# Eleven fill matmuls at two places of the table build, and the first product's matmuls in front in each sum on TensorE

## The chip, the cores and the metric

The kernel runs on one core of one Trainium2 chip. The metric is the device time of one execution in microseconds (us); the median of several runs is compared. The engines are TensorE (PE in the profile, its weight loads PEld), VectorE (DVE), ScalarE (ACT), GpSimd (POOL) and SyncE (SP, which issues most DMAs).

## The reference

Four layers over x of 2048 rows and 512 columns, bf16, two kinds in turn:

```python
x = A_u
x = x + _A_ref(_layernorm(x), A_re, A_im, B_re, B_im, C_re, C_im, log_dt, Dskip)
x = x + _B_ref(_layernorm(x), wqkv, wo)
x = x + _A_ref(_layernorm(x), ...same parameters...)
x = x + _B_ref(_layernorm(x), wqkv, wo)
```

`_A_ref` is a state-space convolution along the rows. For every column d it forms a kernel K[d, l] = Re sum over n of C[d,n] * exp(dt*A[d,n]*l) * dt*B[d,n], with 128 complex modes n and 2048 lags l, multiplies by it with FFTs, and adds u * Dskip. `_B_ref` is attention with 32 heads, in which each row looks at 8 earlier rows, two apart. The convolution kernel K depends on the parameters alone, so it is built once and serves both A layers.

## The kernel before

**The stage that matters here** is the first one, `kgen`, which builds the spectrum of K. The powers exp(dt*A*l) are not formed for 2048 lags. A lag is split as u + 8v, and two tables of complex powers are filled, U (20 lags u) and V (32 lags v), for 128 modes on the partitions. This is done in four quarters c of 128 columns d. The tables have two buffers, U[c % 2] and V[c % 2], so quarter 2 can fill its tables only when quarter 0's were read. A product of U and V on TensorE over the modes then gives K at all lags. It goes through DRAM into another layout (`rows`), and a second matmul with a constant matrix G gives the spectrum, which is stored to DRAM (`kt_scratch`) and loaded later by the convolution (`Kt`).

**Order by hand.** `KGEN` is a string of words, and each word issues a few instructions; every engine carries out its own in the order of the words. A number after the colon is the quarter.

- `U512p:1`, `v8p:0` and the like: one doubling step of a table. VectorE multiplies a part of the table that is filled by a power, `prod[0]` by its real part and `prod[1]` by its imaginary part (both real and imaginary rows r of the source; lines 489, 495, 497), in a scratch ring of 8192 elements that lies in tile Z.
- `%name`: the two products are added or subtracted on VectorE (L507).
- For a step with a p at its end: `+name` adds them on TensorE instead (`sum_pe`, L521 and L522): a matmul of each product with the identity or the negative identity into one PSUM tile `psadd`. `=name` copies the sum into the table on ScalarE (L528, L531). A step of over 512 columns has `+0name`, `+1name` for the two rows r, each of two pieces of at most 512 columns; the others do both rows in one word.
- `v16yn:c`, `v16xn:c`: the last doubling of V, four VectorE multiplications each (L476), into V and a second table `Vsecond`.
- `pcq`: the product of V and U for quarter c and sixteen of its 64 column pairs, q from 0 to 3 (`product`, L561 and, for the skip term, L565). p03 and p02 need `v16yn:0`, p00 and p01 need `v16xn:0`.
- `kcm` copies the product (L572) and, after the second of a quarter, issues the DMAs through DRAM (L580, L583). `scI` is the spectrum matmul (L594, L599), `ocI` and `ecI` its copies and stores (L610, L618, L623, L604).
- `nJ` and `nJa` are the statistics of the first layer norm (L190, L191 on ScalarE, L185 to L187 on VectorE), `qI`, `mI`, `lI`, `bI` the ladder of squared powers, `c0` to `c2` the last lag, `Aa:c`, `Ba:c`, `ua:c` copies that begin a table.
- `w03:n`: a fill. TensorE multiplies the identity by itself, n columns in matmuls of up to 512, into the PSUM tile that p03 will overwrite (`warm`, L548). Nothing reads the result.

A product's place in the scratch ring is written again some steps later. The ring starts anew where a step doesn't fit, so `v8p:1` writes where `v8p:0` had its products: its `prod[0]` has to wait until the sums `+0v8p:0` and `+1v8p:0` have read the old `prod[0]`, and its `prod[1]` the same for the old one.

The tile of a sum comes from a pool of two PSUM buffers (`psg`), shared with the spectrum matmuls; a third sum waits until ScalarE has copied the first out.

After `kgen` come the convolution (transposes, loads of Kt, multiplication on VectorE, inverse), the attention layer, and both again. They are not touched.

Of the kernel before, what the change touches and what calls it, by code (L numbers as in the profile page):

```python
# [305 lines left out]
def a_layer(nc, tc, C, Xg, Ng, kt_dram, layer, Z, es_z, a=None):  # L306
# [24 lines left out]
    def y_rows(g, hf):  # L331
# [17 lines left out]
           "256": (256, (P0 - 2, 1, 4), (0, 6)), "1024": (1024, (P0, 2, 2), (8,)), "512": (512, (P0, 1, 6), (10,))}  # L349
U_AFTER = {"4": (), "2": ("4",), "1": ("2",), "256": ("2",), "1024": ("256",), "512": ("1024", "256")}  # L350
QC = DCH // 2
KGEN = ("m0 q0 b0 x1 l0 m1 q1 x0 t l1 b1 x3 x2 q2 m2 b2 l2 x5 m3 U4p:1 q3 U4:0 l3 b3 %U4:0 u:1 m4 q4 u:0 l4 b4 m5 q5 U2p:0 l5 "
# [18 lines left out]
PLUS = (13,)  # L371
WHOLE = (1, 2, 3, 4, 5, 6)
FIRST_LOADS = [("rows_end", 3), ("rows_end", 3), ("stored", 2, 2), ("stored", 3, 2)]
# [3 lines left out]
def kgen(nc, tc, C, prm, kt_dram, Zf, norm_row, norm_rstd, norm_apply, norm_apply_row, norm_tiles, load_rest, es_a, es_y, open_conv):  # L377
    everything = KGEN.split()
    with ExitStack() as es:
# [64 lines left out]
        def psum():  # L444
            if not late.get("psum"):
                es_t.close()
                late["psum"] = pool("k_psk", 2, space=PSUM), pool("k_psg", 2, es_y, space=PSUM, side="right")
            return late["psum"]
# [65 lines left out]
        def sum_pe(name, c, rs):  # L514
            prod, out, hn, f, size = sums[name, c]
            ps = tiles["+", name, c, rs] = psum()[1].tile([128, 2, 512], F32, name="psadd", tag="psg")
            for r in rs:
                for k, c0 in enumerate(range(0, size, 512)):
                    s = slice(c0, min(c0 + 512, size))
                    b = r if len(rs) == 2 else k  # L520
                    nc.tensor.matmul(ps[:, b, 0:s.stop - c0], C["ident"][:], prod[0][:, r, s], start=True, stop=False)  # L521
                    nc.tensor.matmul(ps[:, b, 0:s.stop - c0], C["ident" if r else "nident"][:], prod[1][:, 1 - r, s], start=False, stop=True)  # L522

        def sum_out(name, c, rs):
            prod, out, hn, f, size = sums[name, c]
# [154 lines left out]
        for c in range(4):  # L680
# [16 lines left out]
            for full in [n for n in everything if n.endswith(f":{c}") and n[0] in "Uv"]:  # L697
                name = full.split(":")[0]
                key = name.rstrip("xypn")
                if key[0] == "U":  # L700
                    needs = (["x5", *free] if key == "U4" else [f"{base['u']}:{c}"]) + [log2[int(key[1:])]] + in_quarter(c, *["U" + k for k in U_AFTER[key[1:]]])
                else:
                    m = int(key[1:])
                    needs = (["b3", "b4", *free] if m == 2 else [f"{base['A']}:{c}", log2[8 * m]]) + ([f"{base['B']}:{c}"] if m > 4 else []) + in_quarter(c, *[f"v{k}" for k in (2, 4, 8) if k < m])
                    if name[-1] == "n":
                        needs += ["y"] + (["prep"] if c % 2 else [])
                word(full, lambda name=name, c=c: step(name, c, sums), *needs)
                if name[-1] not in "pn":
                    word("%" + full, lambda name=name, c=c: sum_dve(name, c), full)
                for rs in ([(0, 1)] if small(name) else [(0,), (1,)]) if name[-1] == "p" else []:  # L710
                    tag = "" if len(rs) == 2 else str(rs[0])
                    word("+" + tag + full, lambda name=name, c=c, rs=rs: sum_pe(name, c, rs), full, "x5")
                    word("=" + tag + full, lambda name=name, c=c, rs=rs: sum_out(name, c, rs), "+" + tag + full)
# [899 lines left out]
```

## Time and profile before

| | |
|---|---|
| median of 3 runs | 438.28 us (436.13 to 438.46) |
| the profiled execution | 439.68 us, its span 437.9 us |
| TensorE, busy share of the span | 87% |
| VectorE | 92% |
| ScalarE | 75% |
| TensorE clock granted, mean | 0.977 |

The span runs from the first instruction to the last, and the time around it is 1.78 us in the profiled execution. A row of the timeline has the start, the duration, engine, line and operation, what is written and read, the count, and in brackets how long the engine had stood idle and what ended that. A matmul's duration includes its way through the array, so it overlaps the next one: the distance of two starts is what it occupies. A row of the windows has the stretch, its length, busy time and number of instructions of each engine, the mean clock granted to TensorE in that stretch (PEclk, 1.00 or 0.50 where nothing changes in it), and the DMA share.

### The profile page before, as it was taken

What the parts mean: (1) busy time and instruction counts of PE and PEld (TensorE: products, weight loads), DVE (VectorE), ACT (ScalarE), POOL (GpSimd) and SP (SyncE); (2) the same over time, 40 slices, a digit from 0 to 9 for tenths busy, and PEclk for the clock granted to TensorE, in tenths of its full rate; (3) what the DMA queues carried; (4) which work ended last, traced back from release to release, by engine and by line L of the source; (5) the groups of instructions that cost most, each with busy time, mean ns of one, the idle gap of its engine ahead of it and who ended that gap; (6) DMA issues with size and microseconds to landing.
All of it is one profiled execution on the core that took longest, in us unless ns stands there. A gap on an engine that the chain in (4) does not pass through costs nothing.

```text
span 437.9 us, 12189 instructions
## 1 busy us (share of the span) xinstructions
PE 379.9 (87%) x5045; PEld 259.3 (59%) x5084; DVE 402.4 (92%) x783; ACT 329.6 (75%) x604; POOL 25.5 (6%) x66
## 2 busy tenths in 40 slices
PE   1176799999989989999997899789899999996995
PEld 1032586676468745686685465367746578784562
DVE  6999989999889969799999999999789999999993
ACT  6999979998989979755665399979969666652442
POOL 5000002001210000020010000000000002020000
PEclk9998779999999999999999899999999999999998
DMA  7900001254889930016043007458100003562022
GB/s 237 419 10 0 1 3 44 74 168 115 250 241 274 297 117 4 1 31 140 3 89 82 0 4 217 168 153 277 57 0 3 1 1 62 110 115 56 1 98 98
DMA packets 25647, 44.06 MB, mean 101 GB/s; under 512 B 7285, under 2 KB 17206, under 8 KB 24950
## 3 DMA queue, kind: packets, MB, share of 16 engines
q1 hardware_dynamic: 22630, 37.30, 29.4%
q0 software_dynamic: 1856, 4.53, 4.4%
q10 hardware_dynamic: 1104, 1.44, 0.9%
q8 instruction: 40, 0.66, 0.7%
q14 instruction: 17, 0.14, 0.1%
HBM read 29.01 MB, written 6.95 MB: 82 GB/s over the span
## 4 chain that ended last, share of the span: by engine, by line
PE 44%; DVE 21%; ACT 21%; issue 7%; DMA 6%; SPq 0%; POOL 0%; DVEq 0%; ACTq 0%; POOLq 0%
PE ps_qk L1170 10%; DVE prodpv L1352 7%; PE ps_v L1257 5%; PE psk L561 4%; DVE prodqk L1220 3%; PE Lp L1242 3%; PE psg L594 3%; ACT xc L272 3%; ACT Z L1426 3%; DVE Z L497 2%; PE pt L254 2%; PE vp L290 2%; PE xp L266 2%; DMA V<-V 2%; ACT X L1406 2%
## 5 line engine op out<-in xcount | busy, mean ns | idle before, releaser
L1352 DVE TENSOR_TENSOR prodpv<-V,Lsb 128x512 bf16<-128x512 bf16 (+1 forms) x124 | 79.4, 701 | 1.2 <-PE po L1362 1.1
L1170 PE MATMUL ps_qk<-xnT,wqk 128*128 128x512 bf16 x256 | 60.3, 379 | 0.0
L1362 PE MATMUL po<-halves,prodpv 128*128 128x64 bf16 x1024 | 38.9, 193 | 7.4 <-DVE prodpv L1352 5.8
L1218 DVE TENSOR_TENSOR prodqk<-qT,N 128x1024 bf16<-128x1024 bf16 (+3 forms) x88 | 42.5, 539 | 2.6 <-ACT N L1173 2.2
L1362 PEld LDWEIGHTS <-prodpv 128*128 128x128 bf16 x1024 | 34.8, 98 | 16.5 <-DVE prodpv L1352 11.1
L279 DVE TENSOR_TENSOR pab<-xc,Kt 128x2048 bf16<-128x2048 bf16 (+1 forms) x34 | 39.2, 1160 | 2.9 <-ACT xc L272 2.8
L1220 DVE TENSOR_TENSOR prodqk<-qT,N 128x512 bf16<-128x512 bf16 (+3 forms) x56 | 40.6, 762 | 0.7 <-ACT N L1173 0.6
L1373 ACT CAST oT<-po 128x512 bf16<-128x512 f32 x32 | 18.3, 595 | 27.4 <-PE po L1362 27.4
L1170 PEld LDWEIGHTS <-wqk 128*128 128x128 bf16 x256 | 23.9, 97 | 23.8
L272 ACT CAST xc<-xp 128x1024 bf16<-128x1024 f32 (+1 forms) x34 | 34.3, 1020 | 4.1 <-PE pt L254 2.8
L299 ACT CAST VT<-vp 128x1024 bf16<-128x1024 f32 (+1 forms) x32 | 33.2, 1052 | 3.1 <-PE vp L290 3.1
L290 PE MATMUL vp<-sb_IC,pab 128*128 128x128 bf16 x512 | 33.8, 219 | 1.2 <-ACT VT L299 0.4
L290 PEld LDWEIGHTS <-pab 128*128 128x128 bf16 x512 | 30.6, 98 | 6.0 <-issue 1.9
L1242 PEld LDWEIGHTS <-prodqk 128*128 128x128 bf16 x1024 | 29.6, 96 | 4.1 <-DVE prodqk L1218 0.6
L1242 PE MATMUL Lp<-sb_bones,prodqk 128*128 128x8 bf16 x1024 | 30.5, 166 | 0.2 <-DVE prodqk L1220 0.2
L1257 PE MATMUL ps_v<-wv,xnT 128*128 128x256 bf16 x256 | 30.4, 272 | 0.0
L521 PE MATMUL psadd<-Z,sb_ident 128*128 128x512 bf16 (+3 forms) x49 | 17.8, 376 | 12.6 <-DVE Z L497 8.2
L1389 PE MATMUL ps_o<-wo_t,oT 128*128 128x512 bf16 x91 | 26.4, 396 | 0.8 <-issue 0.2
L1257 PEld LDWEIGHTS <-xnT 128*128 128x128 bf16 x256 | 24.3, 97 | 3.6
L1173 ACT CAST qT<-ps_qk 128x512 bf16<-128x512 f32 x32 | 18.8, 593 | 7.5 <-PE ps_qk L1170 7.5
L1123 DVE BATCH_NORM_STATS2 ln_stats<-X 128x6 f32<-128x512 bf16 x37 | 23.7, 675 | 0.8 <-ACT X L1447 0.8
L1281 POOL DMA_DIRECT2D V<-V x16 | 8.9, 561 | 255.8 <-ACT V L1264 228.4
(201 smaller groups left out, 854.1 us busy)
## 6 DMA issues: line engine op xcount, KB each, us to landing
Kt<-kt_scratch SPq DMA_DIRECT2D x60, 256.0 KB
kt_scratch<-ks SPq DMA_DIRECT2D x32, 128.0 KB
G<-c_G SPq DMA_DIRECT2D x2, 1536.0 KB
V<-V SPq DMA_DIRECT2D x8, 288.0 KB
X<-in_A_u_dram SPq DMA_DIRECT2D x4, 512.0 KB
F1Tsb<-c_F1T SPq DMA_DIRECT2D x2, 1024.0 KB
V<-V SPq DMA_DIRECT2D x4, 512.0 KB
V<-V POOLq DMA_DIRECT2D x4, 384.0 KB, 7.3
```

The source lines that it names most:

```text
L272: nc.scalar.copy(xc[:, gs].rearrange("q g o l -> q (g o l)"), xp[:].rearrange("q h n -> q (h n)")[:, gs.start * 128:gs.stop * 128])
L279: nc.vector.tensor_tensor(pab[:, gs], xc[:, gs].to_broadcast([128, n, 2, 128]), kt[:, gs], ALU.mult)
L290: nc.tensor.matmul(vp[:, g, :], pab[:, g, ab, :], C["IC"][:, ab, :], start=(ab == 0), stop=(ab == 1))
L299: nc.scalar.copy(dst[..., gs], src[..., gs])
L1170: nc.tensor.matmul(t.ps[:], wqk[:, ct, f0:f0 + 128], x_group(g)[:, :, ct], start=(ct == 0), stop=(ct == 3))
L1218: nc.vector.tensor_tensor(b.pr[:, u:u + 2 * n, 1 - halves_of[0], :], q, cols(kT[i][:, starts[0]:starts[0] + n * 128]), ALU.mult)
L1220: nc.vector.tensor_tensor(b.pr[:, u:u + 2 * n].rearrange("f u a q -> f a u q")[:, ::-1], q.unsqueeze(1).to_broadcast([128, 2, 2 * n, 64]), ...
L1242: nc.tensor.matmul(t.Lp[:, w, u % 2, u // 2, :], b.pr[:, u].rearrange("f a q -> f (a q)"), bones[:], start=False, stop=(t.parts == W // 2 ...
L1257: nc.tensor.matmul(t.ps[:, jj, :], tokens(ct, jp * 2 + jj, c), wv[:, ct, fp * 256:(fp + 1) * 256], start=(jj + ct == 0), stop=(jj == 1 and ...
L1352: nc.vector.tensor_tensor(t.p2[:, c:c + k, 0:nj, :].rearrange("p c j (d h) -> p c j d h", d=DH), m.V2[i // 2][:, c0 + c:c0 + c + k, r0:r0 ...
L1362: nc.tensor.matmul(po[jj // k][:, jj % k, c, :], t.p2[:, c - c0, jj, :], fold, start=(first and c == c0 and jj % k == 0), stop=(last and c ...
L1389: nc.tensor.matmul(t["ps"][:], m.oT[:, ft, j * 128:(j + 1) * 128], wo_t[:, ft, :], start=(added and ft == 0), stop=False)
```

## The change

Two edits.

1. In `KGEN`, `w03:1536` (three matmuls of 512 columns) is put behind `=U256p:0`, ahead of `+0v8p:0`, and `w03:4096` (eight matmuls of 512 columns) behind `U512p:1`, ahead of `p03`. The words around them:

```diff
-... Ba:0 +U256p:0 w03:384 l9 =U1p:1 b10 v8p:0 =U256p:0 +0v8p:0 U1024p:1 Ba:1 +1v8p:0 U1024p:0 ...
+... Ba:0 +U256p:0 w03:384 l9 =U1p:1 b10 v8p:0 =U256p:0 w03:1536 +0v8p:0 U1024p:1 Ba:1 +1v8p:0 U1024p:0 ...
-... v8p:1 b9 +1v8p:1 w03:128 =U1024p:0 =1v8p:1 v16yn:0 +0v8p:1 w03:512 n5a U512:0 m10 q10 %U512:0 n3a =0v8p:1 U512p:1 p03 n9a v16xn:0 p02 n14a +0U512p:1 +1U512p:1 ...
+... v8p:1 b9 +1v8p:1 w03:128 =U1024p:0 =1v8p:1 v16yn:0 +0v8p:1 w03:512 n5a U512:0 m10 q10 %U512:0 n3a =0v8p:1 U512p:1 w03:4096 p03 n9a v16xn:0 p02 n14a +0U512p:1 +1U512p:1 ...
```

2. In `sum_pe` the loop over the two products becomes the outer one. With two matmuls on each product (rows r or pieces of 512 columns), the order was prod[0], prod[1], prod[0], prod[1] and becomes prod[0], prod[0], prod[1], prod[1]. The number of matmuls and what they add stay.

```diff
-            for r in rs:
-                for k, c0 in enumerate(range(0, size, 512)):
-                    s = slice(c0, min(c0 + 512, size))
-                    b = r if len(rs) == 2 else k
-                    nc.tensor.matmul(ps[:, b, 0:s.stop - c0], C["ident"][:], prod[0][:, r, s], start=True, stop=False)
-                    nc.tensor.matmul(ps[:, b, 0:s.stop - c0], C["ident" if r else "nident"][:], prod[1][:, 1 - r, s], start=False, stop=True)
+            for i in range(2):
+                for r in rs:
+                    for k, c0 in enumerate(range(0, size, 512)):
+                        s = slice(c0, min(c0 + 512, size))
+                        nc.tensor.matmul(ps[:, r if len(rs) == 2 else k, 0:s.stop - c0], C["ident" if r or not i else "nident"][:],
+                                         prod[i][:, r if i == 0 else 1 - r, s], start=(i == 0), stop=(i == 1))
```

TensorE gets 22 more instructions (eleven matmuls, eleven weight loads). The order of the other engines is the same.

More of the change, by code (lines that the diff above doesn't have):

```diff
@@ L351 @@
 QC = DCH // 2
-KGEN = ("m0 q0 b0 x1 l0 m1 q1 x0 t l1 b1 x3 x2 q2 m2 b2 l2 x5 m3 U4p:1 q3 U4:0 l3 b3 %U4:0 u:1 m4 q4 u:0 l4 b4 m5 q5 U2p:0 l5 "
[18 rows of a table removed]
+KGEN = ("m0 q0 b0 x1 l0 m1 q1 x0 t l1 b1 x3 x2 q2 m2 b2 l2 x5 m3 U4p:1 q3 U4:0 l3 b3 %U4:0 u:1 m4 q4 u:0 l4 b4 m5 q5 U2p:0 l5 +U2p:0 "
[18 rows of a table added]
 PLUS = (13,)
```

36 rows, old and new, of the table KGEN are left out of this document.

## The prediction

> **What bounds the kernel now.** I read the page first, for the clock, then the table build by windows and by the timelines of PE, DVE and ACT.
>
> ```profile
> span 437.9 us, 12189 instructions
> ...
> PEclk9998779999999999999999899999999999999998
> ```
>
> A slice is 10.95 us, so the three slices with 8, 7, 7 are 33 to 66 us: TensorE's clock was lowered inside the stage that changes. The lowered stretches begin and end on a grid of 3.41 us, so I asked for windows on that grid. Columns: stretch, length, busy time and number for PE, PEld, DVE, ACT, POOL, then the granted clock.
>
> ```profile
> 35.89:39.30 3.41, 1.60 (x8) 0.59 (x7) 3.41 (x7) 3.41 (x8) 0.00 (x0) 1.00 0.00 0
> 39.30:42.71 3.41, 3.04 (x9) 1.07 (x9) 2.48 (x10) 2.82 (x5) 0.00 (x0) 0.50 0.00 0
> 42.71:46.13 3.42, 2.51 (x16) 1.36 (x15) 3.42 (x5) 3.25 (x7) 0.32 (x1) 1.00 0.02 5
> 46.13:49.54 3.41, 0.88 (x5) 0.36 (x4) 3.41 (x6) 3.38 (x8) 0.00 (x0) 1.00 0.00 0
> 49.54:52.95 3.41, 3.10 (x71) 3.02 (x71) 3.41 (x6) 3.31 (x10) 0.00 (x0) 0.50 0.00 0
> 52.95:56.37 3.42, 3.42 (x71) 3.02 (x67) 3.42 (x6) 2.92 (x8) 0.00 (x0) 0.50 0.02 5
> 59.78:63.19 3.41, 3.41 (x121) 3.31 (x121) 2.65 (x8) 3.35 (x9) 0.00 (x0) 1.00 0.03 5
> 72.00:103.00 31.00, 29.85 (x426) 20.17 (x428) 30.54 (x63) 28.52 (x57) 3.72 (x6) 1.00 0.37 107
> 240.70:244.11 3.41, 2.24 (x52) 1.75 (x49) 3.41 (x10) 1.07 (x2) 0.00 (x0) 1.00 0.00 0
> 244.11:247.52 3.41, 3.19 (x11) 1.23 (x11) 3.41 (x6) 0.58 (x1) 0.00 (x0) 0.50 0.00 0
> ```
>
> A window in which PE does little (1.60 us, 0.88 us) is followed by one at half clock. The clock is back after 39.30 to 42.71, a window full of long matmuls, but not after 49.54 to 52.95, nor after 52.95 to 56.37, although PE is busy throughout: there it runs the products, whose matmuls have 40 columns. At full clock the same products hold the clock (59.78 to 63.19). So the drop at 49.54 costs three windows. From 72 to 103 PE and DVE are both almost full, so what comes earlier at 72 has nothing to wait for but each other.
>
> The places where DVE and ACT stand, with what ended it in brackets:
>
> ```profile
> 39.99 1.70 DVE L495 TENSOR_TENSOR Z<-Utab,L 128x256 bf16<-128x256 bf16 x8
> 42.62 2.10 DVE L497 TENSOR_TENSOR Z<-Vtab,Z 128x1792 bf16<-128x1792 bf16 x2 [0.93 <-ACT Vtab L528]
> ...
> 63.28 0.27 DVE L507 TENSOR_TENSOR Vtab<-Z 128x128 bf16<-128x128 bf16 x1 [0.85 <-PE psk L561]
> 63.42 0.69 DVE L656 TENSOR_TENSOR cl<-cb,L 128x1024 bf16<-128x1024 bf16 x1
> 64.27 1.10 DVE L497 TENSOR_TENSOR Z<-Vtab,Z 128x768 bf16<-128x768 bf16 x2 [0.16 <-ACT Vtab L690]
> 66.07 0.76 DVE L497 TENSOR_TENSOR Z<-Utab,Z 128x512 bf16<-128x512 bf16 x2 [0.71 <-ACT Utab L531]
> ...
> 79.31 0.66 DVE L476 TENSOR_TENSOR Vtab<-Vtab,Z 128x960 bf16<-128x960 bf16 x1 [0.42 <-ACT Vtab L528]
> ```
>
> ```profile
> 55.78 0.19 ACT L191 ACTIVATION_READ_ACCUMULATOR n_junk<-X,n_mv 128x1 f32 x1
> 58.70 0.80 ACT L528 CAST Utab<-psadd 128x768 bf16<-128x768 f32 x1 [2.73 <-PE psadd L522]
> ...
> 64.14 0.68 ACT L572 CAST KT<-psk 128x640 bf16<-128x640 f32 x1
> ```
>
> DVE has 3.07 us of waits up to 79.31 (0.93 + 0.85 + 0.16 + 0.71 + 0.42) and ACT one of 2.73 us. All go back to sums and products on PE at half clock.
>
> **Part one: fill and order at 39 us.** PE's rows for `+0v8p:0`, and then for the place of the second fill and for the sums behind p02:
>
> ```profile
> 39.22 0.54 PE L521 MATMUL psadd<-Z,sb_ident 128*128 128x512 bf16 x1 [1.18 <-DVE Z L497]
> 40.13 0.58 PE L522 MATMUL psadd<-Z,sb_nident 128*128 128x512 bf16 x1 [0.37 <-DVE Z L497]
> 40.51 0.52 PE L521 MATMUL psadd<-Z,sb_ident 128*128 128x384 bf16 x1
> 40.83 0.52 PE L522 MATMUL psadd<-Z,sb_nident 128*128 128x384 bf16 x1
> ...
> 46.63 0.38 PE L548 MATMUL psk<-sb_ident 128*128 128x512 bf16 x1
> 49.85 0.57 PE L561 MATMUL psk<-Utab,Vtab 128*64 128x40 bf16 x8 [2.84 <-DVE Utab L507]
> ...
> 55.92 0.61 PE L521 MATMUL psadd<-Z,sb_ident 128*128 128x512 bf16 x1
> ```
>
> At half clock 384 columns occupy 0.32 us (40.51 to 40.83), so 512 take 0.43 and, at full clock, 0.215. DVE's wait of 0.93 is named after ACT, but `v8p:1` overwrites the products of `v8p:0`: its prod[0] has to wait for PE's last read of the old prod[0], the third of four matmuls of `+1v8p:0`. The new order puts that piece of `+0v8p:0` (0.32) into the gap before 40.13, and in `+1v8p:0` it lets the read of prod[0] end one matmul (0.43) earlier: 0.75 of the 0.93 even at half clock. The fill adds 3 x 0.215 = 0.65 us in the 1.18 us gap, whose end is set by DVE; it delays nothing, and would do so only if the gap were below 0.65. It raises PE's busy time in 35.89 to 39.30 from 1.60 to 2.25. Is that enough? 240.70 to 244.11 has 2.24 and was still followed by half clock, but with 52 small matmuls; 42.71 to 46.13 has 2.51 and wasn't. By columns, which I take because the fills are 512 wide, the eight matmuls of 35.89 to 39.30 have 3,072 (summed over their rows) and with the fill 4,608; the sixteen of the window that held have 4,736, the 52 at 240.70 under 3,000. 4,608 is near the one that held, so I take it that the clock holds. Then `+0v8p:0` ends by 40.13 + 0.215 + 0.16 + 0.2 of latency, 40.7, `+1v8p:0` has read prod[0] 0.4 us later, and DVE, done at 41.69 (39.99 + 1.70), no longer waits. Gain on DVE: 0.93 (0.75 without the fill). ACT follows, as its copies there wait for these sums.
>
> **Part two: eight matmuls ahead of p03.** PE is done with its last fill at 46.85 (46.63 + 0.215) and stands 2.84 us until DVE has filled U. Eight matmuls are 8 x 0.215 = 1.72 us at full clock, which the row at 42.71 shows. Both ends of the gap move by part one's 0.93, so 1.1 us stay free. Cover gone (half clock at that place), the fill is 3.44 us and ends 0.6 us behind the tables: that is the most it can cost. PE's busy time in 46.13 to 49.54 becomes about 0.9 + 1.6 = 2.5, as in the window that held.
>
> If the clock holds, p03 and p02, 6.07 us from 49.85 to 55.92 at 71 matmuls in 3.10 us, go at 121 in 3.41 us: a factor of 0.645, 3.9 us, 2.15 saved. The eight matmuls of the two U512 sums behind them (3,072 columns, 512 in 0.43 or 0.215 us) save 1.3 more. So PE has the sums 0.93 + 2.15 + 1.3 = 4.4 us earlier, ahead of ACT: ACT's `=1U512p:1` starts when its own queue is through at 55.97, less the 0.93, at 55.04. ACT gains 2.73 + 0.93 = 3.66, and keeps it to 64.14, the copy after which quarter 0's rows go through DRAM:
>
> ```profile
> 15.55 0.32 SPq L440 DMA_DIRECT2D G<-c_G  x1
> 64.84 11.41 SPq L580 DMA_DIRECT2D rows_scratch<-KT  x4
> ```
>
> ```profile
> 72.81 2.35 PE L594 MATMUL psg<-G,rows 128*128 128x512 bf16 x10 [0.59 <-DMA rows<-rows_scratch]
> ```
>
> So the first spectrum, which waits for these rows, comes up to 3.66 earlier. SP issues nothing between G at 15.55 and the rows, so no transfer of fixed time holds the stage back. DVE's gains: p01 is read 4 us earlier, so its waits of 0.85, 0.16 and 0.71 go, and with the 0.93 it is 2.65 earlier at 66.07; the 0.42 at 79.31 goes because ACT is ahead: 3.07. What is late next is DVE itself, full from then on. In the stretch to 103 the smaller of the two gains counts: 3.1, between 2.3 (if DVE keeps the last 0.42 and a part of the 0.71) and 3.7.
>
> **Part three: the other sums in the new order.** Where both products are ready before PE comes, nothing changes; where PE waits for the second, up to one matmul (0.1 to 0.2 us at full clock) moves ahead of the wait. Turned round, a sum whose buffer is freed late pays nothing, because the count is the same. I take 0, with ends of -0.3 us (two such places) and +0.1.
>
> **The sum.** 439.68 - 3.1 = 436.6 for the profiled execution. The median of the runs, 438.28, is 1.4 lower; the difference is carried over: 435.2.
>
> [...]
>
> **The rivals.**
>
> *The fills don't hold the clock, or only the first place does.* For it: 2.24 us of busy time wasn't enough at 240.70. Against: those were narrow matmuls. What stays is part one, 0.75 to 0.93: 437.4. [...] Chance together 0.13.
>
> *DVE takes only part of it.* If the work for quarter 2 (`U2:2` and on) waits on the ACT copies in their new places, DVE gains about 2: 436.3. Chance 0.14.
>
> *The clock falls in a new gap (the other side).* PE now runs ahead of DVE: p12 waits for `v16yn:1`, and before the sum `+v2p:3` it will stand 1.5 us or more where it was busy throughout (59.78 to 70). If the window to 63.2 or 66.6 is judged too thin, the products behind it don't bring the clock back, as 49.54 to 56.37 show; only the spectra do. Each us at half clock in which PE decides costs 0.5. The gain of 3.1 is used up at 6.2 us, two windows; three windows, as at 49.54, make 10.2 us, 5.1 lost, 2.0 net: 440.3. Against: the sums and spectra among them are wide. Chance 0.10, and 0.05 for one window (436.9).
>
> *Another phase.* The grid need not lie so in each execution. The run of 436.13 may be one where a drop was missed; the changed kernel could gain little against such a run, but is itself at about 435.5. It shifts the comparison, not my number. Windows later in the kernel (240.70) may also fall otherwise, 1.7 us either way.
>
> **How the numbers follow.** Forecast 0.58, half gains 0.14, no hold 0.13, new gap 0.15. About 0.5% (2.2 us) is what a measurement of this kernel can tell from no change, that is 436.1. Of the forecast 0.52 lies below that, of the half gains 0.06, of the others 0.02: faster 0.60. Slower by over 0.5% needs 5.3 us lost, over three windows: 0.09. The rest is 0.31. The range: below, the 3.7 with 1 us of luck in a later window, 433.6; above, the case without hold and the lighter drops, 438.6.
>
> **What would show it.** Right: PEclk 1.00 in all windows from 32 to 72; p03 at about 48.9 and the two products in 3.9 us; DVE's 0.93 at 42.62 and ACT's 2.73 gone; the first spectrum at about 69.5. Wrong: a 0.50 in any window from 39 to 76, p03 waiting behind its fill, or a first spectrum 3 us earlier with PE or DVE standing as long before 103.

## The result, and the profile after

The changed kernel takes 435.65 us (median of 22 runs, 434.2 to 439.73) against 438.28 for the kernel before (22 runs, 436.12 to 439.73): a ratio of 0.9954, interval 0.9937 to 0.9971. Forecast were 435.2 and a range of 433.6 to 438.6. The profiled execution of the changed kernel took 438.22 us and is one of its longest. The forecast number came out, yet one of its two steps is not there and the other worked only in part of the executions. The page shows the first sign: the clock is not full from 33 to 66 us.

```profile
span 436.4 us, 12211 instructions
...
PEclk9998889999999999999999799999999999998999
```

The windows of the same execution, laid on its own grid of 3.41 us (columns as before: stretch, length, busy time and number for PE, PEld, DVE, ACT, POOL, then the granted clock):

```profile
33.99:37.40 3.41, 2.54 (x7) 1.13 (x8) 3.41 (x8) 3.41 (x8) 0.00 (x0) 0.50 0.00 0
...
47.64:51.06 3.42, 2.34 (x66) 1.99 (x65) 3.42 (x6) 3.39 (x8) 0.00 (x0) 1.00 0.00 0
51.06:54.47 3.41, 3.41 (x76) 3.22 (x74) 3.41 (x6) 3.25 (x11) 0.00 (x0) 0.50 0.02 5
54.47:57.88 3.41, 3.19 (x25) 1.84 (x24) 3.34 (x8) 1.61 (x4) 0.00 (x0) 0.50 0.00 0
57.88:61.30 3.42, 3.42 (x117) 3.29 (x115) 3.42 (x9) 3.36 (x9) 0.00 (x0) 1.00 0.02 5
```

The grid lies elsewhere than in the profile of before (edges at 51.06 and 54.47 here against 49.54 and 52.95). The window 47.64 to 51.06 begins just before the fill ends, so it holds the rest of the gap and narrow products. It is busy for 2.34 us and the clock falls all the same, for two windows in place of three. TensorE's timeline of this execution:

```profile
39.49 0.54 PE L521 MATMUL psadd<-Z,sb_ident 128*128 128x512 bf16 x2
40.40 0.54 PE L521 MATMUL psadd<-Z,sb_nident 128*128 128x512 bf16 x2 [0.37 <-DVE Z L497]
...
45.92 2.10 PE L548 MATMUL psk<-sb_ident 128*128 128x512 bf16 x9
49.11 0.40 PE L561 MATMUL psk<-Utab,Vtab 128*64 128x40 bf16 x8 [1.08 <-DVE Utab L507]
...
54.27 0.82 PE L521 MATMUL psadd<-Z,sb_ident 128*128 128x512 bf16 x2
...
71.30 2.35 PE L594 MATMUL psg<-G,rows 128*128 128x512 bf16 x10 [0.83 <-DMA rows<-rows_scratch]
```

The old fill of one and the new of eight matmuls stand as one row of nine (2.10 us), and 1.08 us of the gap stay, as forecast (1.1). p03 starts at 49.11, its first matmuls still at full clock (0.40 for eight, 0.57 before), and p03 with p02 takes 5.16 us to the sum at 54.27; before it was 6.07, forecast 3.9. The first spectrum starts at 71.30, not 69.5. DVE and ACT:

```profile
40.26 1.71 DVE L495 TENSOR_TENSOR Z<-Utab,L 128x256 bf16<-128x256 bf16 x8
41.88 2.09 DVE L497 TENSOR_TENSOR Z<-Vtab,Z 128x1792 bf16<-128x1792 bf16 x2
...
62.62 1.10 DVE L497 TENSOR_TENSOR Z<-Vtab,Z 128x768 bf16<-128x768 bf16 x2 [0.21 <-ACT Vtab L690]
64.39 0.76 DVE L497 TENSOR_TENSOR Z<-Utab,Z 128x512 bf16<-128x512 bf16 x2 [0.66 <-ACT Utab L531]
...
77.80 0.66 DVE L476 TENSOR_TENSOR Vtab<-Vtab,Z 128x960 bf16<-128x960 bf16 x1 [0.59 <-ACT Vtab L528]
```

```profile
55.07 0.19 ACT L191 ACTIVATION_READ_ACCUMULATOR n_junk<-X,n_mv 128x1 f32 x1
57.05 0.80 ACT L528 CAST Utab<-psadd 128x768 bf16<-128x768 f32 x1 [1.79 <-PE psadd L521]
```

The waits of 0.93 and 0.85 are gone, those of 0.16, 0.71 and 0.42 are still there at 0.21, 0.66 and 0.59, and ACT's went from 2.73 to 1.79. The first spectrum is 1.51 us earlier than in the profile of before (71.30 against 72.81) and the span 1.5 shorter (436.4 against 437.9). One pair of profiles doesn't show that this is the change's doing: two further profiles of the kernel before, below, have neither the 0.93 nor the 0.85 and reach the first spectrum at 70.99 and 70.77.

### The profile page after: what moved, and what is told of

It is laid out like the page before. It is cut to its first block, busy times and chain, and to the rows that moved or that the text cites. A ratio compares the mean times of both kernels' runs of the same rounds, so it can differ in the third digit from the quotient of the medians.

```text
span 436.4 us, 12211 instructions
## 1 busy us (share of the span) xinstructions
PE 380.6 (87%) x5056; PEld 261.0 (60%) x5095; DVE 402.5 (92%) x783; ACT 329.4 (75%) x604; POOL 25.3 (6%) x66
## 4 chain that ended last, share of the span: by engine, by line
PE 42%; DVE 23%; ACT 16%; issue 6%; DMA 3%; SPq 0%; DVEq 0%; POOLq 0%; ACTq 0%
PE ps_qk L1170 10%; DVE prodpv L1352 8%; DVE prodqk L1220 4%; PE ps_v L1257 3%; PE Lp L1242 3%; PE psg L594 3%; ACT xc L272 3%; ACT Z L1426 3%; PE pt L254 2%; PE psk L561 2%; PE po L1362 2%; PE vp L290 2%; PE xp L266 2%; PE ps_o L1389 2%; ACT X L1406 2%
## 5 line engine op out<-in xcount | busy, mean ns | idle before, releaser
L1362 PE MATMUL po<-halves,prodpv 128*128 128x64 bf16 x1024 | 40.9, 198 | 6.1 <-DVE prodpv L1352 5.1
L1362 PEld LDWEIGHTS <-prodpv 128*128 128x128 bf16 x1024 | 37.1, 101 | 14.5 <-DVE prodpv L1352 9.3
L521 PE MATMUL psadd<-Z,sb_ident 128*128 128x512 bf16 (+3 forms) x72 | 18.7, 347 | 13.0 <-DVE Z L497 7.7
```

The lines of the kernel that those rows point to most:

```text
L1362: nc.tensor.matmul(po[jj // k][:, jj % k, c, :], t.p2[:, c - c0, jj, :], fold, start=(first and c == c0 and jj % k == 0), stop=(last and c ...
```

## The experiments

Theory: the fill ahead of p03 keeps the clock at full through the products behind it, and only where the grid lies well; that is the whole gain. Rivals: the new order and the first fill free DVE by 0.75 to 0.93 us at 42 us; or the clock falls in a new gap further on and takes a part back. The windows of the theories are the stretches of 3.41 us between the edges of the clock's grid. All ratios are to the kernel before on the same chip.

| version | median us (runs) | ratio and interval |
|---|---|---|
| order alone | 438.11 (12) | 0.9994 (0.9969 to 1.0019) |
| both fills, old order | 435.78 (8) | 0.9942 (0.9919 to 0.9966) |
| order, first fill | 437.94 (12) | 1.0005 (0.9984 to 1.0026) |
| order, second fill | 435.49 (11) | 0.9949 (0.9926 to 0.9972) |
| second fill alone | 435.67 (12) | 0.9953 (0.9929 to 0.9977) |
| whole change again | 434.6 (12) | 0.9941 (0.9917 to 0.9966) |
| kernel before again | 438.02 (12) | 1.0013 (0.9987 to 1.0039) |
| whole change, second fill of 12 matmuls | 435.29 (12) | 0.9948 (0.9926 to 0.9969) |
| the same, and six more matmuls ahead of `+v2p:3` | 435.93 (12) | 0.9963 (0.9939 to 0.9986) |
| the same, old order and no first fill | 436.12 (12) | 0.9969 (0.9945 to 0.9994) |

**Order alone** (both fills out of the changed kernel):

```diff
-... =U256p:0 w03:1536 +0v8p:0 ...  U512p:1 w03:4096 p03 ...
+... =U256p:0 +0v8p:0 ...  U512p:1 p03 ...
```

> The new order in the sums, no fill. Theory A (the order frees the scratch ring for VectorE, the fills hold the clock where the phase of the activity windows allows it): VectorE's 0.93 us wait before v8p:1 shrinks to about 0.2 us or goes, the clock still falls at about 39 and 49.5 us, and the time is 0.7 us lower than before, about 437.6. Theory B (all of the gain is the order's, the fills do nothing that lasts): 2.6 us lower, about 435.7. Theory C (all is the fills'): no change, 438.3.

0.9994: nothing that can be told from no change, as theory C has it. Its windows:

```profile
35.82:39.24 3.42, 1.68 (x9) 0.58 (x6) 3.42 (x7) 3.42 (x7) 0.00 (x0) 1.00 0.00 0
39.24:42.65 3.41, 2.33 (x12) 1.19 (x13) 3.41 (x10) 3.41 (x6) 0.00 (x0) 1.00 0.00 0
...
46.06:49.48 3.42, 0.62 (x19) 0.66 (x18) 3.42 (x7) 3.35 (x9) 0.00 (x0) 1.00 0.00 0
49.48:52.89 3.41, 3.41 (x84) 3.30 (x81) 3.41 (x6) 3.31 (x10) 0.00 (x0) 0.50 0.00 0
```

The grid lies within 0.07 us of that of the profile of before. At 39.24 the clock stays full behind a window with 1.68 us of work and without the first fill, where before it fell behind 1.60: the two outcomes lie 0.08 us of busy time apart here (what parts them is counted further down). At 49.48, without the second fill, it falls.

**Both fills, old order** (`sum_pe` as before):

```diff
-            for i in range(2):
-                for r in rs:
+            for r in rs:
...
```

> Both fills, the old order in the sums. Theory A: VectorE still waits up to 0.4 us before v8p:1 where the clock is full there, and the time is 0.3 to 0.5 us above that of the whole change, about 436.1. Theory B: no change from before, 438.3. Theory C: as the whole change, 435.7.

0.9942: the fills alone do what the whole change does. The clock holds behind 47.12 to 50.53, and in the rest of the table build it falls once, later:

```profile
47.12:50.53 3.41, 2.32 (x63) 1.90 (x61) 3.41 (x6) 3.38 (x7) 0.00 (x0) 1.00 0.00 0
50.53:53.95 3.42, 3.42 (x85) 2.83 (x83) 3.42 (x6) 3.29 (x10) 0.00 (x0) 1.00 0.02 5
64.19:67.60 3.41, 2.56 (x71) 2.24 (x70) 3.41 (x8) 3.23 (x9) 0.77 (x1) 1.00 0.01 1
67.60:71.01 3.41, 3.40 (x11) 1.44 (x11) 3.41 (x10) 1.98 (x6) 0.00 (x0) 0.50 0.18 53
```

```profile
67.61 0.27 PE L521 MATMUL psadd<-Z,sb_ident 128*128 128x128 bf16 x1 [0.85 <-DVE Z L489]
...
69.78 2.94 PE L594 MATMUL psg<-G,rows 128*128 128x512 bf16 x10
```

This is the rival of the new gap, at its place (0.85 us ahead of `+v2p:3`) and for one window. Even so the first spectrum starts at 69.78, 3.0 before that of the profile of before. The execution took 437.24 us, the longest of the eight of this version; what this fall cost is worked out in the part on the rivals.

**One fill each, with the new order:**

```diff
# first fill alone
-... U512p:1 w03:4096 p03 ...
+... U512p:1 p03 ...
# second fill alone
-... =U256p:0 w03:1536 +0v8p:0 ...
+... =U256p:0 +0v8p:0 ...
```

> The new order and the three matmuls at 38 us, without the eight ahead of p03. Theory A: the products p03 and p02 run at half clock in nearly every execution, ScalarE stands 2.5 us ahead of the U512 sums as before, and the time is about 437.2, 1.1 us below before. Theory B: as the whole change, 435.7. Theory C does not say which fill; if the first one, 435.7.

> The new order and the eight matmuls ahead of p03, without the three at 38 us. Theory A: the clock may fall at about 39 us but is back before 46; the second fill delays the fall at 49.5 by one window or prevents it; time about 436.0, 0.3 us above the whole change. Theory B: 435.7, with no difference between any of the runs that have the new order. If the first fill is what counts, 437.5.

1.0005 and 0.9949. The first fill and the order together gain nothing, not the 1.1 us of theory A; the second place carries the gain. But the profile with it has the same fall as that of the changed kernel, behind a window that starts at nearly the same point of the work:

```profile
47.45:50.86 3.41, 2.36 (x75) 2.25 (x75) 3.41 (x7) 3.35 (x9) 0.00 (x0) 1.00 0.00 0
50.86:54.28 3.42, 3.42 (x68) 2.96 (x65) 3.42 (x6) 3.29 (x9) 0.00 (x0) 0.50 0.02 5
```

**The second fill alone, in the kernel before:**

```diff
-... U512p:1 p03 ...
+... U512p:1 w03:4096 p03 ...
```

> The eight matmuls ahead of p03 alone, with the old order in the sums and without the three at 38 us. Theory A2 (the whole gain is this fill's): ratio to before 0.995, as the whole change, 435.5 to 436. If order and first fill are worth what the prediction gave them (0.93 us): 436.5.

0.9953: the whole gain with eight matmuls, in the old order and without the first fill. In its profile the clock holds behind the gap, and the first spectrum starts at 69.04:

```profile
45.85:49.27 3.42, 2.35 (x27) 1.31 (x24) 3.42 (x6) 3.35 (x10) 0.00 (x0) 1.00 0.00 0
49.27:52.68 3.41, 3.41 (x118) 3.28 (x114) 3.41 (x6) 3.31 (x9) 0.00 (x0) 1.00 0.02 5
```

**The two kernels again, in other executions** (no edit; the changed kernel with two profiles more, the kernel before with two):

> The whole change once more, for a second profile of it. The profiled execution so far was among its longest (438.22 against a median of 435.65), with half clock from 51.1 to 57.9 us and the first spectrum at 71.3. Theory A2: most executions do better; this profile has half clock for less than two windows between 46 and 76 us and its first spectrum between 69 and 71. If the fill never holds the clock through the products: two windows again, 71 us or later.

> The same for a third profile: first spectrum between 69 and 71 us by theory A2, 71 or later if the fill only moves the fall by one window in each execution.

> The kernel before once more, so that the granted clock and span of each of its runs are listed. Theory A2 (the activity windows lie anywhere relative to the kernel's start; the second fill alone brings the gain, by making the fall of the clock near 49 us later, rarer or shorter): ratio 1.00, mean granted clock of the runs spread from about 0.965 to 0.985 and lower than the whole change's 0.985, the longer runs with the lower clocks. Rival D (the eight matmuls help by something else than the clock): the clocks are alike, about 0.985.

> The kernel before, for a third profile of it: half clock from the start of p03 on for two or three windows, as in both profiles so far (first spectrum 72.8 and 71.0 us). If its clock holds in some executions, theory A2 overstates what the fill brings.

Windows of the second of these profiles of the changed kernel, then its rows of PE and of ACT:

```profile
48.20:51.61 3.41, 2.99 (x98) 2.89 (x98) 3.41 (x6) 3.33 (x9) 0.00 (x0) 1.00 0.00 0
51.61:55.02 3.41, 3.36 (x73) 2.60 (x70) 3.41 (x5) 3.30 (x9) 0.00 (x0) 1.00 0.02 5
```

```profile
48.62 0.40 PE L561 MATMUL psk<-Utab,Vtab 128*64 128x40 bf16 x8 [1.06 <-DVE Utab L507]
...
52.76 0.50 PE L521 MATMUL psadd<-Z,sb_ident 128*128 128x512 bf16 x2
...
68.75 2.32 PE L594 MATMUL psg<-G,rows 128*128 128x512 bf16 x10
```

```profile
54.61 0.19 ACT L191 ACTIVATION_READ_ACCUMULATOR n_junk<-X,n_mv 128x1 f32 x1
54.70 0.78 ACT L528 CAST Utab<-psadd 128x768 bf16<-128x768 f32 x1
```

Here everything that the prediction drew is there: p03 and p02 in 4.14 us (48.62 to 52.76; forecast 3.9), ACT without a wait ahead of this copy, the first spectrum at 68.75 (69.5). In the other one it starts at 69.45, with p03 and p02 in 4.14 us too. And the kernel before in another execution, its windows, DVE, PE and ACT:

```profile
47.26:50.67 3.41, 1.74 (x56) 1.67 (x56) 3.41 (x6) 3.38 (x7) 0.00 (x0) 1.00 0.00 0
50.67:54.08 3.41, 3.41 (x81) 3.33 (x79) 3.41 (x6) 3.28 (x9) 0.00 (x0) 0.50 0.02 5
54.08:57.50 3.42, 3.20 (x23) 1.74 (x23) 3.35 (x7) 1.48 (x5) 0.00 (x0) 0.50 0.00 0
57.50:60.91 3.41, 3.41 (x116) 3.28 (x115) 3.41 (x9) 3.38 (x8) 0.00 (x0) 1.00 0.00 0
```

```profile
40.08 1.71 DVE L495 TENSOR_TENSOR Z<-Utab,L 128x256 bf16<-128x256 bf16 x8
41.70 2.10 DVE L497 TENSOR_TENSOR Z<-Vtab,Z 128x1792 bf16<-128x1792 bf16 x2
```

```profile
48.93 0.40 PE L561 MATMUL psk<-Utab,Vtab 128*64 128x40 bf16 x8 [2.77 <-DVE Utab L507]
...
70.77 2.35 PE L594 MATMUL psg<-G,rows 128*128 128x512 bf16 x10 [0.42 <-DMA rows<-rows_scratch]
```

```profile
57.03 0.80 ACT L528 CAST Utab<-psadd 128x768 bf16<-128x768 f32 x1 [1.91 <-PE psadd L522]
```

The old order, neither of the two fills, and no wait of 0.93 at 41.70: that wait belonged to the execution whose clock fell at 39.30. ACT's wait, 2.73 there, is 1.91 here and 1.78 in the other repeat. The fall behind the 2.77 us gap belongs to the kernel. All five profiles without the second fill have it, for two windows or three, and their first spectra start at 72.81, 70.99, 70.77, 71.23 and 71.75, on average 71.5. With eight matmuls it is there in two of six; the first spectra are 71.30, 70.64, 69.45, 68.75, 69.04 and 69.78, on average 69.8. The difference of 1.7 us lies within the measured gain, 2.0 by the ratio (438.28 x 0.0046; its interval is 1.3 to 2.8). Rival D, a help that isn't the clock's, would have had alike clocks: the median of the mean granted clock is 0.976 in the twelve repeats of the kernel before and 0.988 in the twelve of the changed kernel.

**What parts the windows.** The prediction weighed its first place by columns. Counted so in all fourteen profiles, on each one's own grid from 28 to 425 us, the cases part where busy time doesn't part them. (The columns of a matmul are counted from its start, 0.417 ns each at full clock, by the 0.16 us of 384 in the second fill alone from 45.15 to 45.31, and 0.833 at half, by the 0.32 us of 384 before from 40.51 to 40.83; a matmul across an edge counts in part on each side.) Full clock was followed by half behind 34 windows, of at most 3,116 columns; of the 1,517 windows behind which it held, eight have fewer than 3,072. At half clock, the 16 windows behind which it stayed low have at most 3,066, and 30 of the 34 behind which it came back have 3,072 or more; each of the four others lacks the record of a 512-column sum that other profiles show there.

| profile, window | PE busy, us | columns | next window |
|---|---|---|---|
| before, 35.89 | 1.60 | 3,030 | half |
| order alone, 35.82 | 1.68 | 3,194 | full |
| changed, 47.64 | 2.34 | 2,985 | half |
| order, second fill, 47.45 | 2.36 | 2,912 | half |
| both fills, old order, 47.12 | 2.32 | 3,039 | full |
| second fill alone, 45.85 | 2.35 | 4,370 | full |
| changed, first repeat, 46.99 | 2.42 | 3,871 | full |
| both fills, old order, 64.19 | 2.56 | 2,938 | half |

This is a count over these fourteen profiles, not an experiment, and windows near 3,070 go against it, as 47.12 does, which held with 3,039. It fits what the products do: at half clock a window of theirs behind which the clock stayed low has at most 3,066 columns, at full clock it has 4,640 (before, 59.78).

**Closing the gaps.** If the falls of the changed kernel come from the 1.1 us that its fill leaves, four matmuls more, and six more at the place of the new gap, should end them:

```diff
# gap closed
-... U512p:1 w03:4096 p03 ...
+... U512p:1 w03:6144 p03 ...
# both gaps: this, and
-... p11 w23:256 %U256:2 v2p:3 ...
+... p11 w23:1792 %U256:2 v2p:3 ...
# both gaps, old order: these two, sum_pe as before, and
-... =U256p:0 w03:1536 +0v8p:0 ...
+... =U256p:0 +0v8p:0 ...
```

> The whole change with twelve matmuls in place of eight ahead of p03, so that TensorE stands 0.2 us instead of 1.05 us before p03 (in the whole change the window with this gap and the first products is just about thin enough to lower the clock: 2.34 us of busy time was followed by half clock, 2.32 in the run with fills only was not). Theory A2: the clock holds through p03 and p02 wherever the window lies, first spectrum at about 69.5 us, time 434.8, 0.8 us below the whole change. Rival E (products of 40 columns lower the clock by themselves whenever a window is full of them): no change from the whole change, 435.6, half clock again from about 51 us. Rival D: 435.6 or longer.

> As the last, and the fill w23:256 after p11 made w23:1792, 0.64 us more of matmuls where the run with fills only stood 0.85 us and had half clock from 67.6 us on. Theory A2: the second fall goes too where it occurred; 434.5, 0.3 us below the run with one gap closed. Rival E: 435.6.

> The twelve and the longer w23, with the old order in the sums and without the three matmuls at 38 us. Theory A2: as the run with both gaps closed and the rest of the change, 434.5 to 434.8, since order and first fill count only in executions where the clock is low at 39 us. The view of the prediction (order and first fill are worth 0.93 us): 435.5.

The clock holds behind p03 in all three profiles. Windows and PE of the first of them:

```profile
46.03:49.44 3.41, 3.22 (x32) 1.74 (x30) 3.41 (x6) 3.35 (x10) 0.00 (x0) 1.00 0.00 0
49.44:52.86 3.42, 3.42 (x116) 3.32 (x114) 3.42 (x6) 3.32 (x9) 0.00 (x0) 1.00 0.02 5
```

```profile
48.75 0.40 PE L561 MATMUL psk<-Utab,Vtab 128*64 128x40 bf16 x8 [0.19 <-DVE Utab L507]
...
68.87 2.32 PE L594 MATMUL psg<-G,rows 128*128 128x512 bf16 x10
```

The gap is 0.19 us, and the first spectra are at 68.87, 69.11 and 69.18, on average 69.05: 0.8 us ahead of the six with eight matmuls. The times don't show it (0.9948, 0.9963, 0.9969, against 0.9941 to 0.9954 for the whole change; 0.8 us would be 0.0018 less), and the forecasts of 434.8, 434.5 and 434.5 to 434.8 are missed. That the clock holds speaks against rival E. The last two versions differ by order and first fill alone and by 0.0006, so these are again worth nothing that shows. In the three profiles the lead reaches the attention (first `ps_qk` matmul at 164.42, 164.65 and 164.72, on average 165.54 for the six) and is mostly lost up to the second attention (163.66 against 163.01 us), in a stage with a fall of its own at 236 to 244 us. Whether that is chance or the rule isn't shown: the mean clock of these versions is higher (medians 0.9915 to 0.993 against 0.985 and 0.988) and their time isn't lower. No version is shown to beat the changed kernel.

## Why the prediction came out, point by point

**Part one (0.93, or 0.75 by the order) is the step that failed.** Order with first fill measured 1.0005, order alone 0.9994. The mechanism on DVE was read from one execution, in which the clock happened to fall at 39.30; in the other two profiles of the kernel before it didn't, and DVE didn't wait there. So the step was a term of the profiled execution and not of the median, and the sum should not have carried it over. Whether the order gives its 0.75 in executions whose clock is low at 39 was not separated; at the median it is too rare or too small to see: of the seven profiles without the first fill, one has the clock low at 39. The clock also held without the first fill, in order alone, behind 3,194 columns. The choice of columns over busy time was right. p03 came at the forecast 48.9 (48.62 to 49.11), but by luck: without the second fill it starts at 48.92 to 49.07 in the four other profiles, so the 0.93 that the forecast took off was not the change's.

**Part two is the right mechanism with a size off.** The fill alone measures 0.9953. Its terms where the clock holds: p03 and p02 in 4.14 or 4.15 us (forecast 3.9), the first spectrum at 68.75 to 69.78 (69.5). "The clock holds" was taken as a yes, and is a share: four of six profiles. The reason, as far as the runs show it, is the 1.1 us that the fill leaves (with 0.18 or 0.19 us left, behind twelve matmuls, the clock held in three profiles of three): "about 2.5 us busy, as in the window that held" assumed the window at 46.13 to 49.54, which contains the fill whole, but where a window begins as the fill ends it holds the gap and narrow products. The second place was also weighed by busy time, and by that the cases do not part (2.34 and 2.36 fell; 2.32, 2.35 and 2.42 held); by columns the two that fell are the two lowest of the six, 2,985 and 2,912. By the start of the window, counted back from p03, these six do: falls for 1.47 and 1.20 us (47.64 before 49.11, 47.45 before 48.65), none for 2.80, 2.01, 1.54 and 0.42. From these six, falls fill between 0.27 (1.47 - 1.20) and 1.12 us (1.54 - 0.42) of a grid of 3.41, an estimate of a twelfth to a third of the executions if every phase is alike; two of six is the upper end.

**What becomes of the gain.** "What comes earlier at 72 has nothing to wait for" is right: between the profile of before and the first repeat of the changed kernel the first spectrum is 3.36 us earlier, and TensorE's first `ps_qk` matmul of the attention 3.38 (165.01 against 168.39). In eleven of the fourteen profiles the way from the one to the other takes 95.53 to 95.58 us, in the others 95.89, 96.16 and 96.36. The upper end, ACT's 3.66, was even passed in the execution with 68.75 (4.06), where no wait of DVE is left from 38 to 82 us; its span is 4.3 shorter than that of the profile of before (433.6 against 437.9).

**The sum.** 3.1 forecast, 2.63 measured by the medians, 2.0 by the ratio. Three errors all make the forecast too large: the 0.93 of part one, full success for part two, and a profiled execution of the kernel before that loses more than its other two (72.81 at the first spectrum, not 70.77 and 70.99). In these DVE's waits up to 79 us come to 1.12 and 1.15, not 3.07, and ACT's to 1.91 and 1.78, not 2.73. By the profiles the gain is 1.7 on average; that the medians of the runs differ by 2.63, near the 3.1, is in part luck. So the number was better than its working.

**Part three** at 0 agrees with the order alone at 0.9994 (-1.4 to +0.8 us) and can't be told closer.

**The rivals.** That the fills do not hold is true in two profiles of six and wrong as a whole: 0.9953 for a fill in a gap of 2.8 us. Half clock followed a gap of 2.77 us with a window of 1.74 us busy (kernel before, third profile) as well as one of 1.08 us with a window of 2.34 (changed kernel). The new gap exists (67.60 in both fills, old order), in one of the five profiles whose clock holds through p03 and p02 and in which this gap isn't filled. That only the spectra bring the clock back was the author's estimate: here it is back behind a window with eight matmuls of sums and the first of the spectrum (67.60 to 71.01), and in the profile of before behind one of sums and products without a spectrum (56.37 to 59.78). As a share of the executions the new gap doesn't decide the median. Its price, half a microsecond per microsecond at half clock, is somewhat high: that execution reaches the first `ps_qk` matmul at 165.94, the three others with eight matmuls and no fall from p03 up to there at 164.28, 164.60 and 165.01, so one window of 3.41 us goes with about 1.3 us, 0.4 per microsecond. Behind p03 it is 0.3: 166.53 and 166.88 with two half windows (6.83 us), 2.1 later. Over all stages it is less. Over 225 runs of all these kernels the time rises by about 1.8 us for each 0.01 that the mean granted clock is lower; 0.01 of 437 us is 8.7 us at half clock (437 x 0.01 / 0.5), so about 0.2 per microsecond, an average that is no price for a single place. *Another phase*, which was given no chance of its own, is what happened: it decides the difference between the two profiled executions, and it was named as shifting the comparison alone, while it also cancels part one. Its reach of 1.7 us either way for windows later in the kernel fits the later stage (last section): 113.56 against 115.24 and 115.3 us.

## What to carry to other kernels

A wait that one profile shows behind a lowered clock is a term of that execution until a second profile shows it again; profile the kernel before more than once when the grid of the clock lies differently from profile to profile (edges at 49.54 and 50.67 us here). The fill paid here (0.9953 for eight matmuls) where TensorE stood 2.8 us ahead of long runs of matmuls of 40 columns, which held a full clock (121 of them in 3.41 us before, 59.78) but did not win back a lowered one at once (two windows of 71 before, from 49.54 on); place a fill so that no window on any phase is left with the gap alone (with 0.18 or 0.19 us left the clock held in three profiles of three, with 1.0 to 1.1 in four of six, though the times do not tell the two apart). Weigh a window by columns and not by busy time alone: here 1.68 us with 3,194 columns held and 2.56 us with 2,938 fell. Price a lowered clock from profiles of the same stage with and without the fall (0.3 to 0.4 us per microsecond here) rather than by the stretched matmuls, a part of which lies beside other work.

## What the runs showed of the hardware that was not expected

- The clock's grid of 3.41 us lies elsewhere relative to the work from profile to profile (an edge at 49.54 and at 50.67 in two of the kernel before, at 51.06, 50.40 and 51.61 in three of the changed one), and the same kernel (the changed one) takes 434.2 to 439.73 us. Time and mean granted clock are correlated at -0.80 over 225 runs; the median of the mean clock is 0.977 before and 0.985 after.
- A part of the spread lies in a later stage that no edit touches. From the first `ps_qk` matmul of the first attention to the first transpose of the second convolution the kernel before takes 115.24, 113.56 and 115.3 us in its three profiles; the longer ones have one half window from 244.1 on and two from 238.4, the shorter one only one, at 236.9. No version has a fill there.
- In the fourteen profiles columns part the windows behind which the clock fell (at most 3,116 in 3.41 us, 34 windows) from those behind which it held (3,072 or more in all but eight of 1,517), where busy time does not (1.68 us of work held; 2.34, 2.36 and 2.56 fell). That this is what the clock goes by was not tested by a run that sets the columns. The start of the window relative to p03 separates the six profiles with eight matmuls too (falls for 1.20 and 1.47 us ahead of it, none for 0.42, 1.54, 2.01 and 2.80); that this is by how much of the fill and of the products the window holds is the author's estimate.
